# The first MLP product of the last 24 weight tiles as seven 64x64 block products instead of eight

## The chip, the core and the metric

The kernel runs on one core of a Trainium2 chip. TensorE (PE) multiplies, VectorE (DVE), ScalarE (ACT) and GpSimd (POOL) do elementwise work, SyncE (SP) issues most DMA transfers. The metric is the device time of one execution in microseconds (us). The kernel before takes 259.07 us, the median of three runs (259.07, 259.70 and 259.07).

## The reference

```
phi(x)   = outer(S1 x, S2 x), 64 features for each token and head
attn     = (phi(q) . sum phi(k) v) / (phi(q) . sum phi(k) + 1e-6)     # 4 batches, 4 heads, 1088 tokens, head size 32
x        = attn as 4352 tokens by 128
h        = x @ w_in                       # 4352x128 by 128x2048
g        = 0.5 h (1 + erf(h / sqrt 2))
out      = g @ w_out                      # 4352x2048 by 2048x128
```

All of it is in float32. The two products of the MLP (x by w_in, g by w_out) are by far the largest part of the arithmetic. This document calls them the first and the second product.

## The kernel before, in words

**Chunks, tiles, blocks and steps.** The 4352 tokens are eight chunks of 512 tokens (0 to 7) and a last one of 256 (chunk 8, the rests of the four batches). The 2048 hidden features are 16 tiles of 128, and four tiles make a block. One pass of the main loop (L1163) is a step: it makes one hidden tile of one chunk. From chunk 2 on, step t makes tile t mod 16 of chunk t div 16, so step 96 opens chunk 6, step 104 is the middle of chunk 6, step 112 opens chunk 7 and step 128 opens chunk 8. Chunks 0 to 7 with 16 tiles are the 128 w_in tiles of the title.

**What one step does.** `hidden` (L715) multiplies a w_in tile by the chunk's transposed x, as two matmuls of 64 output columns each (the array as two column tiles, "128*64" in the profile) into one of two PSUM banks (`h_ps`). ACT applies GELU to that bank (L728) and writes the tile into the chunk's block. After the last tile of a block `token_sums` (L764) forms four sums of 128x512 of pieces of the block on POOL, each about 1.28 us.

**The second product is already done as seven products for eight.** This is a Strassen-Winograd scheme on a 2x2 block form: halves of the 256 tokens by halves of 128 output columns, over pairs of tiles. Its token side is what `token_sums` makes, its weight side (`T`, `channel_sums`, L749) is made once. `two_products` (L794) issues one pair of products of 128*64 tiles and 256 columns each, into the chunk's two PSUM banks `acc` (`o_ps`). A block has seven such pairs; they are spread over the steps after the block by the table `products` (L1133 to L1161). `drain` (L812) takes the two banks apart once a chunk's products are done: two ACT copies and seven DVE operations, all of which read PSUM and have at most one operand in SBUF. `combine` (L837) adds SBUF to SBUF (L841, L842), and `store` (L860) transposes on DVE and issues the output's DMAs on SP.

**Order.** Every engine runs its instructions in the order in which the text emits them: the loop at L1217 to L1223 ties each instruction to the one before it on its engine. So on DVE, an operation of an earlier step is never overtaken by one of a later step, however late its own inputs are. Within a step the order is: `drain` of that step, `hidden`, the `slots` (functions placed with `at(t, ...)`), `store`, then that step's `products`. For chunk 5 `drain` stands at step 101 and `store` at step 107. `last_attends` at step 95 makes the x of chunks 6, 7 and 8.

**PSUM.** There are eight banks: two `h_ps`, two `o_ps`, and four `w_ps` (two pairs, used by the attention part, which is done by step 95 but for the accumulators of chunk 8).

The lines that tie the order:

```
    last = {}
    for ins in nc.cur_bb.bb.instructions:
        if ins.engine in last:
            tc.add_manual_dep(ins, last[ins.engine].name,
                              mybir.DependencyInfo(mybir.DependencyClass.NoSync, mybir.DependencyReason.DATA),
                              reason="order of the text")
        last[ins.engine] = ins
```

Of the kernel before, what the change touches and what calls it, by code (L numbers as in the profile page):

```python
# [8 lines left out]
FP = mybir.dt.float32  # L9
U32 = mybir.dt.uint32  # L10
AX = mybir.AluOpType
ACT = mybir.ActivationFunctionType
# [4 lines left out]
def kernel(  # L17
# [17 lines left out]
    nc = tc.nc  # L35
    pe, dve, act, pool, sp = nc.tensor, nc.vector, nc.scalar, nc.gpsimd, nc.sync
# [5 lines left out]
    NF = d_ff // 128  # L42
# [5 lines left out]
    CW = JC * 128  # L48
    G = 128 // 32
    NCH = J // JC  # L50
    C = D + 1
    LAG = 2
    NMAIN = B * NCH
    NB = 4
# [6 lines left out]
    att = ctx.enter_context(tc.tile_pool(name="att", bufs=2))  # L61
    mlp = ctx.enter_context(tc.tile_pool(name="mlp", bufs=2))
# [4 lines left out]
    def work_banks():  # L67

        return wps.tile([128, 2, CW], FP, name="w_ps")
# [7 lines left out]
    def hidden_bank():  # L77
        return hps.tile([128, CW], FP, name="h_ps")

    def out_bank():  # L80
        return ops.tile([128, CW], FP, name="o_ps")
# [5 lines left out]
    pieces = list(zip(CUTS, CUTS[1:]))  # L87
# [4 lines left out]
    main = {(n, b): big.tile([128, H, J, D], FP, name=f"{n}_{b}") for n in "kv" for b in range(B)}  # L92
    q_sb = [big.tile([128, H, JC, D], FP, name=f"q_{n}") for n in range(NMAIN)]
    w_in_sb = [big.tile([d_model, c1 - c0], FP, name=f"w_in{i}") for i, (c0, c1) in enumerate(pieces)]
# [42 lines left out]
    def block(dtype=U32):  # L137

        b = big.tile([128, NB, 512], U32, name="block", bufs=3)
        return b if dtype == U32 else b.bitcast(dtype)  # L140
# [46 lines left out]
    for i, s in enumerate((S1, S2)):  # L187
        s, e = words(s)
# [328 lines left out]
    qT, qp, xT = {}, {}, {}  # L517
# [13 lines left out]
    A, B_of = {}, {}  # L531
# [174 lines left out]
    g_of, o_of = {}, {}  # L706

    def w_tile(w, fi):
        i = max(i for i, (c0, c1) in enumerate(pieces) if c0 <= fi * 128)
        at = fi * 128 - CUTS[i]  # L710
        return w[i][:, at:at + 128]
# [3 lines left out]
    def hidden(n, fi, by_halves=False):  # L715
        W = width[n]
        ps = first_banks.pop((n, fi)) if (n, fi) in first_banks else hidden_bank()
        w = w_tile(w_in_sb, fi)
        for rows in (slice(0, 64), slice(64, 128)) if by_halves else (slice(0, 128),):
            if (n, fi) not in begun:  # L720
                pe.matmul(ps[rows, :W], lhsT=w[:, rows], rhs=xT[n][:, :W], start=True, stop=True)  # L721
        if n < NCH and fi < USUAL:
            g_of[n, fi] = mlp.tile([128, CW], FP, name="g", bufs=4)
        else:
            if fi % NB == 0:
                blocks[n, fi // NB] = block(FP)
            g_of[n, fi] = blocks[n, fi // NB][:, fi % NB]
        act.activation(out=g_of[n, fi][:, :W], in_=ps[:, :W], func=ACT.Gelu)  # L728

    def first_hidden(n, half):  # L730
# [4 lines left out]
        for i in range(parts):  # L735
# [5 lines left out]
    blocks, sums, acc = {}, {}, {}  # L741
    T = {}
    HW = CW // 2
    NPAIR = NF // 2

    PLACE = {"1": (0, 0, 0), "2": (0, 0, HW), "3": (1, 0, 0), "5": (1, 0, HW),
             "4": (0, 1, 0), "6a": (0, 1, HW), "7": (1, 1, 0), "6b": (1, 1, HW)}
# [16 lines left out]
    def token_sums(n, b):  # L764

        g = blocks[n, b].rearrange("p (e two) (half x) -> p e two half x", two=2, half=2)
        a11, a21, a12, a22 = (g[:, :, k, h] for k in range(2) for h in range(2))
        s = {}
        for j, (name, dtype) in enumerate((("bits_a", U32), ("bits_e", U32), ("bits_low", FP), ("bits_m", FP))):
            t = mlp.tile([128, LC], dtype, name=name, bufs=3 if dtype == U32 else 2)  # L770
            s[j + 1] = (t if dtype == FP else t.bitcast(FP)).rearrange("p (e x) -> p e x", e=2)
        pool.tensor_sub(out=s[3], in0=a11, in1=a21)  # L772
        pool.tensor_add(out=s[1], in0=a21, in1=a22)  # L773
        pool.tensor_sub(out=s[2], in0=s[1], in1=a11)  # L774
        pool.tensor_sub(out=s[4], in0=a12, in1=s[2])  # L775
        sums[n, b] = s

    def factor(n, b, name, e):

        k = 2 * b + e  # L780
        if name in "12":
            fi = 2 * k + int(name) - 1
            return g_of[n, fi][:, 0:HW], w_tile(w_out_sb, fi)[:, 0:64]
        if name == "3":
            return sums[n, b][4][:, e], w_tile(w_out_sb, 2 * k + 1)[:, 64:128]
        if name == "4":
            return g_of[n, 2 * k + 1][:, HW:], T[4][:, k]
        j = {"5": 1, "6": 2, "7": 3}[name[0]]
        return sums[n, b][j][:, e], T[j][:, k]

    def first_block(n):
        return USUAL // NB if n < NCH else 0

    def two_products(n, b, i):  # L794
# [8 lines left out]
        for name, e in zip(two[:2], two[2:]):  # L803
# [3 lines left out]
            pe.matmul(acc[n][bank][half * 64:(half + 1) * 64, col:col + HW], lhsT=fixed, rhs=moving,  # L807
                      start=opens and e == 0 and name in "4715", stop=b == NF // NB - 1, skip_group_check=True)

    drained = {}  # L810

    def drain(n):  # L812
# [79 lines left out]
    bank = work_bank()  # L892
# [74 lines left out]
    def at(t, f, *a):  # L967
        slots[t].append(lambda: f(*a))
# [161 lines left out]
                at(t + 10, turn_first_kv)  # L1130


    products = {t: [] for t in range(len(steps) + LAG)}  # L1133
    done = {t: [] for t in range(len(steps) + LAG + 1)}
    drains = {t: [] for t in range(len(steps) + LAG + 1)}
    for t, (n, fi) in enumerate(steps):
        if n < NCH and fi < USUAL:
            products[t + LAG].append((project, n, fi))
            if fi == USUAL - 1:
                slots[t + LAG + 1 + 2 * n].append(lambda n=n: take_usual(n))  # L1140
        elif n == NMAIN:
            at_ = max(t + LAG, (n * NF + 5) if fi < 3 else (n * NF + 6) if fi < 5 else 0)
            if fi < NF - 4:
                products[at_].append((project, n, fi))
            if fi == NF - 1:

                products[at_] += [(project, n, NF - f, (i,)) for f, i in ((4, 0), (3, 0), (2, 0), (4, 1), (1, 0), (3, 1),
                                                                          (2, 1), (1, 1))]
                done[at_ + 1].append(n)
        elif fi % NB == NB - 1:  # L1150
            b = fi // NB
            opens = b == first_block(n)
            late = int(n < NCH or n == NCH and opens)
            for later, pairs in ((3, 3), (4, 2), (5, 2)) if opens else ((2, 2), (3, 2), (4, 1), (5, 2)):
                later += late
                for i in range(pairs):
                    products[t + later].append((two_products, n, b, len([p for q in products.values() for p in q
                                                                        if p[:3] == (two_products, n, b)])))
            if b == NF // NB - 1:
                drains[t + 6 + late].append(n)  # L1160
                done[t + 12].append(n)  # L1161

    for t in range(len(steps) + LAG):  # L1163
        if t < 4:

            hidden(0, t)
            if t == 1:
                w_out[0].low_words()
                w_out[0].exponents()
                w_out[0].finish()  # L1170
                w_out[1].fields()
            if t == 2:
                w_out[1].low_words()
            if t == 3:
                banks = work_banks()
                numerators_by_token(1, halves(banks), range(JC))
                w_out[1].mantissas(by_pool=True)
                w_out[1].exponents()
                divide(1, banks, range(JC), by_head_pair=False)
                w_out[1].signs()  # L1180
                w_out[1].product()
                project(0, 0)
                project(0, 1, cols=slice(0, 256))
                turn_half(1, 0, work_bank(), by_act)
                project(0, 1, cols=slice(256, 512))
                turn_half(1, 1, work_bank(), by_dve)
            continue
        if t == 4:
            first_hidden(1, 0)
            for f, *a in products[t]:  # L1190
                f(*a)
            first_hidden(1, 1)
        for n in drains[t]:
            drain(n)
        sooner = t == NMAIN * NF
        if sooner:
            for f, *a in products[t]:
                f(*a)
        if t < len(steps):
            n, fi = steps[t]  # L1200
            hidden(n, fi, by_halves=t >= 18 and (n < NMAIN or fi < 5))
        if t < len(steps) and steps[t][0] < NMAIN and steps[t][1] % NB == NB - 1:
            n, b = steps[t][0], steps[t][1] // NB
            if b >= first_block(n):
                token_sums(n, b)
        for f in slots[t]:
            f()
        for n in done[t]:
            store(n)
        if t != 4 and not sooner:  # L1210
            for f, *a in products[t]:
                f(*a)
# [4 lines left out]
    last = {}  # L1217
# [36 lines left out]
```

## Time and profile before

| what | us |
|---|---|
| median of three runs | 259.07 |
| the profiled execution, first to last instruction (its span) | 257.9 |
| PE busy in it | 253.1 |
| POOL busy | 163.6 |
| DVE busy | 151.1 |
| ACT busy | 115.2 |
| step 101 (chunk 6, tile 5) starts on PE | 192.93 |
| step 104 starts on PE | 197.66 |
| step 128 (chunk 8) starts on PE | 237.26 |

The profile is one execution. All times in it are counted from its first instruction. The profiled execution's own time is its span and what lies around it (launch and the last transfer's end): the median is 1.2 us above the span. A matmul of float32 shows as two records, one for each of its passes, and a record is longer than the time until the next one may start, because matmuls are pipelined. "PEld" is the loading of weights, which runs beside the matmuls.

### The profile page before, as it was taken

What the parts mean: (1) busy time and instruction counts of PE and PEld (TensorE: products, weight loads), DVE (VectorE), ACT (ScalarE), POOL (GpSimd) and SP (SyncE); (2) the same over time, 40 slices, a digit from 0 to 9 for tenths busy, and PEclk for the clock granted to TensorE, in tenths of its full rate; (3) what the DMA queues carried; (4) which work ended last, traced back from release to release, by engine and by line L of the source; (5) the groups of instructions that cost most, each with busy time, mean ns of one, the idle gap of its engine ahead of it and who ended that gap; (6) DMA issues with size and microseconds to landing.
All of it is one profiled execution on the core that took longest, in us unless ns stands there. A gap on an engine that the chain in (4) does not pass through costs nothing.

```text
span 257.9 us, 5770 instructions
## 1 busy us (share of the span) xinstructions
PE 253.1 (98%) x2335; PEld 135.5 (53%) x2335; DVE 151.1 (59%) x313; ACT 115.2 (45%) x224; POOL 163.6 (63%) x173
## 2 busy tenths in 40 slices
PE   8989999999999999999999999999999999999995
PEld 7846444354444545444444455455544444445794
DVE  3786888969699997590178986399307000700330
ACT  4665777433626332543335332533444334433442
POOL 3313006799968778587758775787758777877300
PEclk9999999999999999999999999999999999999999
DMA  6459747751000101102000002000200200020020
GB/s 203 143 156 375 181 117 174 211 131 15 4 0 13 29 3 23 20 8 35 3 0 3 0 10 37 0 1 3 41 3 5 38 0 1 7 36 0 3 41 20
DMA packets 29594, 13.48 MB, mean 52 GB/s; under 512 B 21888, under 2 KB 27776, under 8 KB 29568
## 3 DMA queue, kind: packets, MB, share of 16 engines
q1 hardware_dynamic: 29392, 13.05, 20.2%
q8 instruction: 18, 0.29, 0.5%
q10 hardware_dynamic: 176, 0.07, 0.1%
q14 instruction: 8, 0.07, 0.1%
HBM read 10.88 MB, written 2.23 MB: 51 GB/s over the span
## 4 chain that ended last, share of the span: by engine, by line
PE 93%; SPq 2%; DMA 2%; DVE 1%; issue 0%; ACT 0%
PE h_ps L721 45%; PE o_ps L807 33%; PE o_ps L858 5%; PE w_ps L855 3%; DMA small<-in_moe_w_in_dram 2%; PE w_ps L437 1%; PE w_ps L578 1%; PE w_ps L633 1%; SPq L132 1%; PE h_ps L737 1%; SPq L100 1%; PE w_ps L977 1%; PE w_ps L656 0%; SPq L118 0%; PE w_ps L467 0%
## 5 line engine op out<-in xcount | busy, mean ns | idle before, releaser
L721 PE MATMUL h_ps<-xT,w_in 128*64 128x512 f32 (+3 forms) x514 | 136.9, 576 | 0.0
L728 ACT ACTIVATE block<-h_ps 128x512 f32<-128x512 f32 (+1 forms) x128 | 73.1, 571 | 117.2 <-PE h_ps L721 115.3
L721 PEld LDWEIGHTS h_ps<-xT,w_in 128*64 128x64 f32 (+1 forms) x514 | 41.9, 142 | 30.5 <-issue 11.6
L807 PE MATMUL o_ps<-block,w_out 128*64 128x256 f32 x224 | 57.5, 379 | 0.0
L772 POOL TENSOR_TENSOR bits_low<-block 128x512 f32<-128x512 f32 x28 | 36.0, 1286 | 27.7 <-ACT block L728 27.7
L807 PEld LDWEIGHTS o_ps<-block,w_out 128*64 128x64 f32 x224 | 30.5, 137 | 38.0 <-issue 27.5
L773 POOL TENSOR_TENSOR bits_a<-block 128x512 f32<-128x512 f32 x28 | 35.8, 1278 | 11.8 <-ACT block L728 11.8
L822 DVE COPY sums<-o_ps 64x256 f32<-64x256 f32 x8 | 3.3, 417 | 60.6 <-PE o_ps L807 60.6
L774 POOL TENSOR_TENSOR bits_e<-bits_a,block 128x512 f32<-128x512 f32 x28 | 36.1, 1288 | 2.2
L775 POOL TENSOR_TENSOR bits_m<-block,bits_e 128x512 f32<-128x512 f32 x28 | 35.9, 1282 | 2.2
L807 PE MATMUL o_ps<-bits_a,small 128*64 128x256 f32 x112 | 28.8, 379 | 0.0
L807 PE MATMUL o_ps<-bits_low,small 128*64 128x256 f32 x112 | 28.8, 379 | 0.0
L807 PE MATMUL o_ps<-block,small 128*64 128x256 f32 x112 | 28.8, 379 | 0.0
L807 PE MATMUL o_ps<-bits_m,w_out 128*64 128x256 f32 x112 | 28.7, 379 | 0.0
L807 PEld LDWEIGHTS o_ps<-block,small 128*64 128x64 f32 x112 | 15.2, 137 | 17.9 <-issue 10.8
L807 PE MATMUL o_ps<-bits_e,small 128*64 128x256 f32 x112 | 17.0, 383 | 0.0
L858 PE MATMUL o_ps<-g,w_out 128*128 128x512 f32 (+1 forms) x34 | 16.5, 572 | 0.0
L807 PEld LDWEIGHTS o_ps<-bits_m,w_out 128*64 128x64 f32 x112 | 15.3, 137 | 0.0
L807 PEld LDWEIGHTS o_ps<-bits_a,small 128*64 128x64 f32 x112 | 15.2, 137 | 0.0
L807 PEld LDWEIGHTS o_ps<-bits_low,small 128*64 128x64 f32 x112 | 15.2, 137 | 0.0
L590 DVE STREAM_TRANSPOSE w_ps<-w_ps 128x512 f32<-128x512 f32 (+1 forms) x7 | 4.8, 687 | 17.1 <-ACT xT L644 12.7
L807 PEld LDWEIGHTS o_ps<-bits_e,small 128*64 128x64 f32 x112 | 7.7, 137 | 10.6 <-issue 8.8
(195 smaller groups left out, 303.7 us busy)
## 6 DMA issues: line engine op xcount, KB each, us to landing
block<-in_moe_w_in_dram SPq DMA_DIRECT2D x3, 512.0 KB, 11.3
block<-in_moe_w_out_dram SPq DMA_DIRECT2D x3, 512.0 KB, 14.7
k<-in_k_dram SPq DMA_DIRECT2D x12, 128.0 KB, 2.9
v<-in_v_dram SPq DMA_DIRECT2D x12, 128.0 KB, 3.5
q<-in_q_dram SPq DMA_DIRECT2D x24, 64.0 KB, 2.1
out_dram<-oT SPq DMA_DIRECT2D x21, 64.0 KB, 2.2
k<-in_k_dram SPq DMA_DIRECT2D x2, 256.0 KB, 2.8
q<-in_q_dram SPq DMA_DIRECT2D x2, 256.0 KB, 3.9
```

The source lines that it names most:

```text
L100: eng.dma_start(out=main[n, b][:, heads], in_=src_of[n][b, heads, 0:MAIN, :].rearrange("h (p j) d -> p h j d", j=J))
L590: dve.transpose(out=tok, in_=ps[:, :, :H2])
L721: pe.matmul(ps[rows, :W], lhsT=w[:, rows], rhs=xT[n][:, :W], start=True, stop=True)
L728: act.activation(out=g_of[n, fi][:, :W], in_=ps[:, :W], func=ACT.Gelu)
L772: pool.tensor_sub(out=s[3], in0=a11, in1=a21)
L773: pool.tensor_add(out=s[1], in0=a21, in1=a22)
L774: pool.tensor_sub(out=s[2], in0=s[1], in1=a11)
L775: pool.tensor_sub(out=s[4], in0=a12, in1=s[2])
L807: pe.matmul(acc[n][bank][half * 64:(half + 1) * 64, col:col + HW], lhsT=fixed, rhs=moving, start=opens and e == 0 and name in "4715", stop ...
L822: dve.tensor_copy(out=N[lo, 0, one], in_=a0[lo, one])
L855: pe.matmul(o_of[n][i][:, :128], lhsT=g[:, i * 128:(i + 1) * 128], rhs=w_tile(w_out_sb, fi), start=first, stop=final)
L858: pe.matmul(o_of[n][:, cols], lhsT=w_tile(w_out_sb, fi), rhs=g[:, cols], start=first, stop=final)
```

## The change

For six blocks, chunk 6's blocks 2 and 3 and the four of chunk 7, the first product is also made as seven 64x64 block products for eight: halves of w_in's 128 rows by halves of a tile pair's columns. All matmuls of both products in these six blocks are on 64x64 tiles of the array.

- `swap_weights` (step 64): ten DMAs on SP copy w_in with its upper and lower 64 partitions swapped. `weight_sums` (steps 93, 94, 98, 98, 99): four DVE additions for each of the five pieces of w_in, all from SBUF to SBUF, 12 of them of 128x256 and eight of 128x128.
- `swap_x` (step 96, chunks 6 and 7): two DMAs on SP each. `x_sums` (chunk 6 at step 102, chunk 7 at step 103): five DVE additions of 128x256 each, SBUF to SBUF.
- `seven_group` replaces four steps of `hidden`. It goes twice (k = 0 and 1) over: seven rounds, each of a hidden block product on one half of the rows (both column halves) and a second product's half on the other half of the rows, of the block two before (`outs_with`). The first four rounds hold the seven hidden products. `pair_ones` copies product 1 on ACT, `pair_sums` adds the seven up with four DVE operations (three of 128x512, one of 128x256) into SBUF, and `pair_gelu` applies GELU to 128x1024.
- The seven products lie in one set of six PSUM banks (the two `h_ps`, the four `w_ps`). Products 3 and 4 of both k share one bank.
- `drain_apart` takes chunk 6's accumulators apart: three ACT copies and one DVE addition release the banks; five more DVE additions (SBUF to SBUF) wait in the list `between`, of which two are emitted after each `pair_sums`.
- The second products of chunk 7's blocks 2 and 3, and those of chunk 8, move to later steps; the drain of chunk 7 moves from step 133 to 137.

```
+    def quarter_products(n, b, names, es, rows):
...
+            pe.matmul(acc[n][bank][half * 64:(half + 1) * 64, col:col + HW], lhsT=fixed[rows], rhs=moving[rows],
+                      start=first, stop=b == NF // NB - 1, skip_group_check=True)
+            ins = nc.cur_bb.bb.instructions[-1]
+            if was not in (None, rows.start):
+                tc.add_manual_dep(ins, seen[0], ..., reason="the other rows' products of this bank")
...
+    def weight_sums(i):
...
+        dve.tensor_add(out=s1, in0=w[:, :, 1], in1=o[:, :, 1])
+        dve.tensor_sub(out=s3, in0=w[:, :, 0], in1=w[:, :, 1])
+        dve.tensor_sub(out=s2, in0=s1, in1=o[:, :, 0])
+        dve.tensor_sub(out=s4, in0=w[:, :, 0], in1=s2)
+    def swap_x(n):
+        xs[n] = mlp.tile([128, CW], FP, name="g", bufs=4)
+        for to, of in ((LO, HI), (HI, LO)):
+            sp.dma_start(out=xs[n][to], in_=xT[n][of])
+    def x_sums(n):
...
+        dve.tensor_sub(out=t[:, 1], in0=sb, in1=sa)
+        dve.tensor_sub(out=t[:, 2], in0=b, in1=t[:, 1])
+        dve.tensor_sub(out=t4, in0=a, in1=t[:, 2])
+        dve.tensor_sub(out=t[:, 0], in0=b, in1=a)
+        dve.tensor_sub(out=t[:, 3], in0=sb, in1=b)
+        XS[n] = {"1": a, "2": a, "3": b, "4": t4, "5": t[:, 0], "6": t[:, 2], "7": t[:, 3]}
+    def pair_product(n, b, k, name):
+        rows, p = pair_rows(k, name), 2 * b + k
+        x, to = XS[n][name], seven[k][name]
+        for e in range(2):
...
+            pe.matmul(to[e * 64:(e + 1) * 64], lhsT=w[rows, e * 64:(e + 1) * 64], rhs=x[rows], start=True, stop=True)
+    def pair_sums(n, b, k, one):
...
+        dve.tensor_add(out=c[:, 0::3], in0=ps["26"], in1=one[:, None, :].broadcast_to([128, 2, HW]))
+        dve.tensor_add(out=u, in0=ps["57"], in1=c[:, 3:4].broadcast_to([128, 2, HW]))
+        dve.tensor_add(out=c[:, 3], in0=ps["57"][:, 0], in1=u[:, 1])
+        dve.tensor_add(out=c[:, 1:3], in0=ps["34"], in1=u)
+    def seven_group(n, b, m, mb):
...
+        for k, (one, two) in enumerate(((LO, HI), (HI, LO))):
+            first = hid(k, "157") + outs([B0] + Bs, one)
+            second = hid(k, "2634") + outs(A, two)
+            both = list(zip(first, second))
+            for i, x in enumerate(both[:4]):
+                for f, *a in x if k == 0 else x[::-1]:
+                    f(*a)
+                if i == 0:
+                    p1 = pair_ones(k)
+            if k == 0:
+                held_gelu()
+            else:
+                pair_gelu(n, b, 0, c)
+            c = pair_sums(n, b, k, p1)
+            for _ in range(2):
+                if between:
+                    between.pop(0)()
+            for x in both[4:]:
...
+        after.append(lambda: (pair_gelu(n, b, 1, c), token_sums(n, b)))
+    def drain_apart(n):
...
+        act.copy(out=A0, in_=a0)
+        act.copy(out=C[lo, 0], in_=a1[hi])
+        act.copy(out=N[hi, 0, one], in_=a1[hi, one])
+        dve.tensor_add(out=C[lo, 1], in0=a1[lo], in1=C[lo, 0])
...
+    outs_with = {(6, 2): (6, 0), (6, 3): (6, 1), (7, 0): (6, 2), (7, 1): (6, 3), (7, 2): (7, 0), (7, 3): (7, 1)}
+    at(64, swap_weights)
+    for i, t in ((3, 93), (4, 94), (0, 98), (1, 98), (2, 99)):
+        at(t, weight_sums, i)
+    for n in range(NMAIN - 2, NMAIN):
+        at(96, swap_x, n)
+        at(102 + n - 6, x_sums, n)
...
+                for later, pairs in ((6, 2), (7, 2), (8, 1), (9, 2)):
...
+                    drains[137].append(n)
+                    done[139].append(n)
```

## The prediction

> **What bounds the kernel now.** I read first the page's busy times and its chain of work, then the timeline of PE, DVE and POOL around step 101, where the change begins to differ.
>
> ```profile
> PE 253.1 (98%) x2335; PEld 135.5 (53%) x2335; DVE 151.1 (59%) x313; ACT 115.2 (45%) x224; POOL 163.6 (63%) x173
> ...
> PE 93%; SPq 2%; DMA 2%; DVE 1%; issue 0%; ACT 0%
> ```
>
> PE never rests, and 93% of the chain is PE: a matmul less is time less, as long as nothing makes PE wait. So the question is who may make it wait. The stretches just before the change and within it:
>
> ```profile
> 182.90:193.10 10.20, 10.20 (x128) 5.46 (x128) 0.02 (x1) 5.08 (x10) 6.86 (x7) 1.00 0.17 27
> 199.50:235.50 36.00, 36.00 (x248) 17.55 (x246) 4.99 (x10) 14.13 (x24) 27.92 (x23) 1.00 0.10 16
> ```
>
> The columns are the stretch, then busy PE, PEld, DVE, ACT, POOL. DVE looks free (0.02 of 10.2 us, 4.99 of 36), POOL is 67% and 78% busy. But POOL's and DVE's adds are not independent. From the timelines of POOL and DVE:
>
> ```profile
> 149.22 1.28 POOL L774 TENSOR_TENSOR bits_e<-bits_a,block 128x512 f32<-128x512 f32 x1
> 150.58 1.33 POOL L775 TENSOR_TENSOR bits_m<-block,bits_e 128x512 f32<-128x512 f32 x1
> ...
> 149.71 1.06 DVE L841 TENSOR_TENSOR sums<-sums 64x256 f32<-64x256 f32 x1
> 150.79 1.40 DVE L842 TENSOR_TENSOR sums<-sums 64x256 f32<-64x256 f32 x1
> ```
>
> A DVE add of two SBUF operands that starts while a POOL sum runs ends 0.27 us after that sum's end (150.50 to 150.77, 151.91 to 152.19); free of POOL the same line takes 0.42 (at 245.70). So beside a busy POOL, DVE gets one such add per POOL sum, every 1.41 us. Adds that read PSUM are not held: L823 has 0.68 beside POOL.
>
> **The gain.** One pair of 256 columns takes 0.43 us of PE (L807 at 192.07, 192.50, 192.93). A block costs four tiles of 0.86 and seven pairs of 0.43, 6.45 us. In the change it is 14 rounds of four 64x64 matmuls. If a round takes 0.43, a block takes 6.02, and six blocks save 2.6 us. Do four small tiles run abreast?
>
> ```profile
> 182.86 1.09 PE L633 MATMUL w_ps<-q_pT,kz 64*32 64x256 f32 x32
> ```
>
> These are 32 records on eight 64x32 tiles; 1.09 us less the last one's tail of 0.17 is 0.92, against 0.86 for two full-speed rounds. They do, and I take 0.43. The Trainium skill, TensorE: Matmul & The Clock Gate (Packing small matmuls, measured speedup), speaks against this: packing four row tiles gave 3.07 times, not four. Were a round 4/3.07 longer, 84 rounds would cost 11 us more. This row packs rows and columns without that loss, so the rule gets no term. The change of tile shape costs 0.1 us twice (the gap ahead of L633, 182.76 to 182.86).
>
> **DVE's preparation, the largest term.** It all stands in DVE's text order: store of chunk 4 (ends 182.92), 20 weight sums, drain of chunk 5, five x sums of chunk 6, five of chunk 7, then the first `pair_sums`. All 30 preparing adds have two SBUF operands.
>
> ```profile
> 182.21 0.71 DVE L869 STREAM_TRANSPOSE oT<-sums 128x512 f32<-128x512 f32 x1
> 193.15 0.42 DVE L822 COPY sums<-o_ps 64x256 f32<-64x256 f32 x1 [10.22 <-PE o_ps L807]
> ...
> 189.95 1.27 POOL L772 TENSOR_TENSOR bits_low<-block 128x512 f32<-128x512 f32 x1 [2.32 <-ACT block L728]
> 191.67 1.27 POOL L773 TENSOR_TENSOR bits_a<-block 128x512 f32<-128x512 f32 x1 [0.45 <-ACT block L728]
> ```
>
> Weight sums: from 182.92 to 187.9 POOL has four sums, and DVE gets five adds. POOL then rests until 189.95: five more adds at 0.44 (256 columns) or 0.31 (128). Ten are left, and POOL now has eight sums, one after the other but for one gap at 191.3: both blocks of chunk 6. One add per sum and one in the gap, so the last ends after the eighth sum, 191.67 + 7 x 1.41 = 201.5, plus an add of 0.44: 202. Unhindered they would take 12 x 0.44 + 8 x 0.31 = 7.8 us and end at 190.7. Then the drain (193.15 to 196.31 before, 3.2 us) ends at 205.3 (196.3 unhindered). POOL is by then out of work, so the x sums run at 0.44: product 5's operand, the fourth, is there at 207.1, the fifth at 207.5, those of chunk 7 at 209.7.
>
> PE gets there much earlier. The pairs of chunk 6's block 0 leave steps 102 to 104, so steps 101 to 103 are three bare tiles: 192.93 + 3 x 0.86 = 195.51. Round 0 needs no sums. Round 1 needs product 5: PE waits from 195.94 to 207.2, 11.3 us. Rounds 1 to 6 and two of k = 1 bring it to 210.6; round 2 of k = 1 overwrites the bank of products 3 and 4, which the last add of `pair_sums` reads. That chain (three at 0.68, one at 0.43, gaps: 2.6 us) starts behind the x sums at 209.7 and ends at 212.3: another 1.8 us. Entry: **+13.1**. Unhindered by POOL: x sums from 196.3, wait until 198.2 (2.2 us), chain from 200.9 to 203.5 (1.9): +4.1.
>
> A second rule: the same page of the Trainium skill (The HAM clock gate) halves PE's clock after an idle window of 3.4 us. This profile grants full speed in all its slices, but its first padding matmuls (L890) take 656 ns against 398 for a warm one of that size (L737). By the rule the first four rounds after the wait would take double, 1.7 us more, and PE would reach round 2 of k = 1 at 212.3 instead of 210.6. By either the sum is the same, since DVE's chain ends at 212.3.
>
> **The steady state.** A half (k) is seven rounds, 3.01 us. ACT copies product 1 by 1.0 us after the half's start, DVE's chain runs from 1.06 to 3.66, and the next half's round 2 comes at 3.87. That holds with 0.1 to 0.2 us to spare; every further 0.4 us of DVE work in a half fits, and what is more delays PE one for one. If a handover costs 0.3 more than I think, each of ten halves loses 0.2: bounds 0 to +2; I take 0. GELU of 1024 columns (1.02 us by 385 ns for 256 and 598 for 512) and the copies fill half of ACT. The change adds a wait: the first second-product of a half on each bank waits for that copy, with all later rounds behind it on PE; it stands in round 3, at 1.29, so it has 0.3 us to spare, and ACT's GELU of the half before starts only behind the copy. POOL's four sums (5.4 us with gaps) fit in a block's 6.02, and their readers come two blocks later.
>
> **Other DVE work in the halves.** The store of chunk 5 (step 107) comes behind `pair_sums` of block 2: two SBUF adds and a transpose of 0.71, 1.65 us with POOL idle (it waits for GELU), less the room: **+1.0** (up to +2 beside POOL). The drain of chunk 6: ACT's copies 0.58, 0.58, 0.40, then the DVE add 0.68 release the second bank 2.2 us after the group, which wants it at 1.72: +0.45. The copy of product 1 queues behind these three copies, so the DVE chain is 1.1 late: +0.5 in the next half. Of the five waiting adds two come after each `pair_sums`, and POOL is then at work on chunk 7's block 1: 1.35 and 1.40 instead of 0.44 each. The next chain is late by that much less the room, +2.35; the next two adds and the last find POOL nearly idle: +0.55. Sum **+3.9** (+2.0 if POOL holds none of them).
>
> **Moved at no cost, and what covers it.** SP's ten swaps at step 64 and four at step 96 issue at 0.65 each (L884: 1.30 for two), land in about 2.1, and delay SP's store DMAs by 2.6 us at step 96; nobody on PE waits for stores. If they were late, chunk 6's x sums start later than 190, still far before DVE gets to them. ACT's queue: 128 GELUs become 104 and 12 wide ones, less work. POOL's sums move behind the wide GELU (`held_gelu`): if that came late, pairs wait two blocks on; the cover is 0.6 us. The later pairs of chunks 7 and 8 are as many rounds as before. The end is PE's second products of chunk 8, DVE's drain of chunk 7 at step 137 is 10 us ahead of it.
>
> **Sum.** -2.6 + 0.2 (two changes of tile shape) + 13.1 + 1.0 + 3.9 = +15.6 on a span of 257.9, so 273.5; the median was 1.2 above the span: **274.7 us**. Measurements of this kernel tell no change from one below 0.3%, about 0.8 us.
>
> **Rivals.**
> 1. DVE is late but POOL does not hold its preparing adds, because POOL loses the turns instead. For it: at 181.75 a DVE add kept its 0.42 and the POOL sum took 1.39. Against it: both adds at 149.71. Price: entry 4.1, store 1.0, drain 2.0: 259.07 - 2.4 + 7.1 = 263.8.
> 2. Faster: DVE does the x sums before chunk 5's drain, that is, its order is not the text's. It decides from this point: product 5's operand ready by 195.9. Then the entry costs nothing, and the rest hides if the adds are spread: 259.07 - 2.4 = 256.7. For it: x is on hand from 185.4 and DVE idle for 10 us. Against it: the loop that ties each instruction to the one before.
> 3. The small tiles lose a quarter or the spare 0.2 us is not there: DVE's lateness is then partly hidden under slower rounds, but the steady state adds 3 to 5: 278.
>
> **How the numbers follow.** Forecast (270 to 277) 0.54, rival 1 (261 to 269) 0.22, rival 2 0.17, rival 3 (above 277) 0.05, and 0.02 for no difference. The range 261 to 278 leaves out rival 2, the case of no difference and part of rival 3, 0.2 in all; its ends are rival 1 with its store and drain cheaper, and the forecast with +2 of steady state and +1 of store. Faster is rival 2, 0.17; same 0.02; slower 0.81.
>
> **What would show it.** PE idle of about 11 us near 196 released by a DVE sum of x, and a smaller one near 211 released by the last add of `pair_sums`; L822 of chunk 5 near 202 instead of 193; weight sums of 1.3 to 1.4 us beside POOL; rounds of 0.43 elsewhere; small PE waits after step 107 and in chunk 7's blocks 2 and 3. I am wrong if DVE has finished the x sums near 196, if the adds take 0.44 beside POOL, or if records of 64*64 lie 0.5 us apart.

## The result, and the profile after

The kernel after takes 271.97 us (median of four runs, 271.22 to 272.86), against 259.07 for the kernel before in the same measurement: ratio 1.049, with an interval of 1.0465 to 1.052. It is 12.9 us slower; 274.7 was forecast. The profiled execution is the quickest of the four, 271.22 with a span of 269.4.

PE's slices, its granted clock and the chain of work on the page of the kernel after:

```profile
PE 255.5 (95%) x2751; PEld 146.9 (55%) x2751; DVE 199.1 (74%) x390; ACT 117.9 (44%) x225; POOL 164.6 (61%) x173
...
PE   8999999999999999999999999999908999989995
...
PEclk9999999999999999999999999999977999999999
...
PE 72%; DVE 18%; issue 4%; SPq 2%; DMA 2%; ACT 1%; DVEq 0%; ACTq 0%
```

DVE, with 1% of the chain before, now holds 18%. One slice of PE is empty (each is 6.7 us), the clock is short of full in it and in the slice behind it, and one more slice near the end of the six blocks is short of full. What PE waited for, in total, times, and the longest:

```profile
PE w_ps L896 <- DVE k L870: 6.9, 1, 6.9
PE h_ps L896 <- DVE v L912: 1.2, 1, 1.2
PE h_ps L896 <- DVE k L912: 0.8, 2, 0.6
```

L896 issues a hidden block product. L870 makes the token operand of product 5. L912 is the last add of `pair_sums`. So the large wait is the forecast one, at another size, and the forecast second wait on `pair_sums` in block 2 of chunk 6 is not in the list.

A half (one k, seven rounds) is measured from the start of its product 1 to the start of the next half's. Seven rounds at the predicted 0.43 are 3.01 us. Halves are named (chunk, block) and k. The first start is at 195.28, and the last half ends where step 128 begins, near 245.5.

| half | (6,2) 0 | (6,2) 1 | (6,3) 0 | (6,3) 1 | (7,0) 0 | (7,0) 1 | (7,1) 0 | (7,1) 1 | (7,2) 0 | (7,2) 1 | (7,3) 0 | (7,3) 1 |
|---|---|---|---|---|---|---|---|---|---|---|---|---|
| us | 11.81 | 2.98 | 3.34 | 3.86 | 3.33 | 2.99 | 3.32 | 2.99 | 3.96 | 3.24 | 4.91 | 3.5 |
| over 3.01 | 8.80 | 0 | 0.33 | 0.85 | 0.32 | 0 | 0.31 | 0 | 0.95 | 0.23 | 1.90 | 0.5 |

The excess is 14.1 us (the undisturbed halves are 0.02 to 0.03 under 3.01). The blocks themselves save 2.6 (84 rounds in place of six times 6.45), so 11.5 is left, which is the whole difference of the two spans (269.4 less 257.9). Outside these halves two small amounts cancel: this execution reaches step 101 0.41 us sooner than the profiled one before (192.52 against 192.93), a lead that it has from its first steps on, and it loses about as much at the change of tile shape into the first half and behind step 128.

DVE before and in the large wait, from its timeline (start, length):

```profile
189.55 1.41 DVE L855 TENSOR_TENSOR v<-w_in,v 128x128 f32<-128x128 f32 x1
...
191.29 0.28 DVE L854 TENSOR_TENSOR v<-k,q 128x128 f32<-128x128 f32 x1
...
192.77 0.41 DVE L852 TENSOR_TENSOR k<-w_in,q 128x256 f32<-128x256 f32 x1
...
196.05 1.37 DVE L855 TENSOR_TENSOR v<-w_in,v 128x256 f32<-128x256 f32 x1
197.34 0.41 DVE L990 COPY sums<-o_ps 64x256 f32<-64x256 f32 x1
...
200.40 1.11 DVE L867 TENSOR_TENSOR k<-g 128x256 f32<-128x256 f32 x1
201.54 0.42 DVE L868 TENSOR_TENSOR k<-xT,k 128x256 f32<-128x256 f32 x1
202.00 0.42 DVE L869 TENSOR_TENSOR g<-xT,k 128x256 f32<-128x256 f32 x1
202.34 0.41 DVE L870 TENSOR_TENSOR k<-xT 128x256 f32<-128x256 f32 x1
...
205.05 0.69 DVE L909 TENSOR_TENSOR k<-w_ps,q 128x512 f32<-128x512 f32 x1
```

The weight sums run until 197.4, then comes the drain of chunk 5, which was at 193.15 before, then the x sums, and only then `pair_sums`. POOL's sums beside the weight sums:

```profile
189.54 1.27 POOL L772 TENSOR_TENSOR bits_low<-block 128x512 f32<-128x512 f32 x1 [2.04 <-ACT block L728]
191.26 1.44 POOL L773 TENSOR_TENSOR bits_a<-block 128x512 f32<-128x512 f32 x1 [0.45 <-ACT block L728]
192.77 1.54 POOL L774 TENSOR_TENSOR bits_e<-bits_a,block 128x512 f32<-128x512 f32 x1
```

PE on either side of its wait:

```profile
195.56 0.38 PE L896 MATMUL w_ps<-xT,w_in 64*64 64x256 f32 x2
...
202.81 0.69 PE L896 MATMUL w_ps<-k,k 64*64 64x256 f32 x2 [6.87 <-DVE k L870]
```

A matmul of the same shape has 0.38 before the wait and 0.69 behind it. Product 5 was due 0.43 behind product 1, at 195.71; it came 7.1 later, and the six rounds from there to 207.09 took 4.28 instead of 2.58. 7.1 and 1.7 are the 8.8 of this half. Three stretches by engine (stretch, then busy PE, PEld, DVE, ACT, POOL, granted clock, DMA share, GB/s) show the clock in numbers:

```profile
195.00:203.00 8.00, 1.13 (x14) 0.40 (x16) 7.78 (x14) 1.00 (x3) 6.07 (x5) 0.77 0.00 0
203.00:211.00 8.00, 8.00 (x122) 6.84 (x122) 6.61 (x14) 1.56 (x3) 0.00 (x0) 0.81 0.01 2
211.00:246.00 35.00, 32.67 (x552) 24.05 (x548) 29.42 (x50) 15.30 (x23) 25.31 (x20) 1.00 0.06 10
```

In the first, DVE is busy for 7.78 of 8 us and PE for 1.13: the bound of this stretch has gone from PE to DVE. In the second PE is busy throughout, but at 0.81.

### The profile page after: what moved, and what is told of

It reads as the page before. It is cut to its first block, busy times and chain, and to the rows that moved or that the text cites. A ratio compares the mean times of both kernels' runs of the same rounds, so it can differ in the third digit from the quotient of the medians.

```text
span 269.4 us, 6735 instructions
## 1 busy us (share of the span) xinstructions
PE 255.5 (95%) x2751; PEld 146.9 (55%) x2751; DVE 199.1 (74%) x390; ACT 117.9 (44%) x225; POOL 164.6 (61%) x173
## 4 chain that ended last, share of the span: by engine, by line
PE 72%; DVE 18%; issue 4%; SPq 2%; DMA 2%; ACT 1%; DVEq 0%; ACTq 0%
PE h_ps L721 29%; PE o_ps L807 20%; PE o_ps L1026 5%; PE o_ps L823 4%; PE w_ps L1023 3%; PE w_ps L896 2%; PE h_ps L896 2%; DMA small<-in_moe_w_in_dram 2%; PE w_ps L437 1%; DVE v L854 1%; PE w_ps L578 1%; DVE q L910 1%; DVE k L852 1%; DVE q_f L610 1%; DVE k L853 1%
## 5 line engine op out<-in xcount | busy, mean ns | idle before, releaser
L721 PE MATMUL h_ps<-xT,w_in 128*64 128x512 f32 (+3 forms) x426 | 112.2, 569 | 0.0
L728 ACT ACTIVATE block<-h_ps 128x512 f32<-128x512 f32 (+1 forms) x104 | 58.6, 565 | 93.1 <-PE h_ps L721 89.7
L721 PEld LDWEIGHTS h_ps<-xT,w_in 128*64 128x64 f32 (+1 forms) x426 | 34.8, 143 | 27.8 <-issue 11.4
L807 PE MATMUL o_ps<-block,w_out 128*64 128x256 f32 x176 | 45.2, 379 | 0.0
L807 PEld LDWEIGHTS o_ps<-block,w_out 128*64 128x64 f32 x176 | 24.0, 137 | 29.0 <-issue 20.7
L823 PE MATMUL o_ps<-block,w_out 64*64 64x256 f32 x96 | 23.7, 386 | 0.0
L807 PE MATMUL o_ps<-block,small 128*64 128x256 f32 x88 | 22.7, 380 | 0.0
L807 PE MATMUL o_ps<-bits_a,small 128*64 128x256 f32 x88 | 22.6, 380 | 0.0
L1026 PE MATMUL o_ps<-g,w_out 128*128 128x512 f32 (+1 forms) x34 | 16.5, 572 | 0.0
L823 PEld LDWEIGHTS o_ps<-block,w_out 64*64 64x64 f32 x96 | 13.1, 138 | 0.5
L823 PE MATMUL o_ps<-bits_a,small 64*64 64x256 f32 x48 | 13.1, 395 | 0.0
```

What stands on the lines that cost most here:

```text
L1026: pe.matmul(o_of[n][:, cols], lhsT=w_tile(w_out_sb, fi), rhs=g[:, cols], start=first, stop=final)
```

## The experiments

What had to be told apart: whether the large wait belongs to the weight sums beside POOL, to the x sums, or to both; what the clock costs; whether the 0.3 us in the first halves is a wait of DVE or a slower array; and what sets the end of chunk 6's drain. Nine kernels were run; their ratios are to runs of the kernel before on the same chip (medians 259.25 to 259.5). Halves are given only where they differ from the table above.

### Weight sums earlier

```
-    at(64, swap_weights)
-    for i, t in ((3, 93), (4, 94), (0, 98), (1, 98), (2, 99)):
+    at(46, swap_weights)
+    for i, t in ((3, 62), (4, 62), (0, 62), (1, 62), (2, 62)):
```

> The swaps of w_in move to step 46 and all 20 weight sums to step 62, where DVE is idle for 12 us; the x sums and the drain of chunk 5 stay. Theory A (text order on DVE, and an add of two SBUF operands waits out a POOL sum): the drain of chunk 5 starts at about 192.7 instead of 197.3 and ends at 195.9, but the x sums now fall beside POOL's sums of chunk 6's block 1, which last to 200.2, so the fourth is ready only at about 200.4 instead of 202.7, and the wait for product 5's operand is still 4 to 5 us; 1.5 to 2.5 us less than the changed kernel, about 270. Rival (POOL does not hold the adds; DVE is merely late by the weight sums' own length): the fourth x sum is ready at 198, the wait is 2 us, the clock stays up, and the time falls by 5 us or more, to 267 or less. Rival (the x sums wait for their DMA): no change.

Measured: 272.39 us, ratio 1.050 (1.048 to 1.0516): the expected 1.5 to 2.5 us did not come. The chain in question is in DVE's timeline and PE's waits:

```profile
194.51 0.42 DVE L990 COPY sums<-o_ps 64x256 f32<-64x256 f32 x1 [10.22 <-PE o_ps L807]
...
197.70 0.83 DVE L867 TENSOR_TENSOR k<-g 128x256 f32<-128x256 f32 x1
198.56 1.37 DVE L868 TENSOR_TENSOR k<-xT,k 128x256 f32<-128x256 f32 x1
199.96 1.37 DVE L869 TENSOR_TENSOR g<-xT,k 128x256 f32<-128x256 f32 x1
201.25 1.48 DVE L870 TENSOR_TENSOR k<-xT 128x256 f32<-128x256 f32 x1
```

```profile
PE w_ps L896 <- DVE k L870: 5.1, 1, 5.1
...
PE o_ps L807 <- DVE sums L991: 1.2, 1, 1.2
```

The drain now starts as soon as PE has finished chunk 5's last second product, and the x sums follow at 197.70 instead of 200.40. But POOL is not done with its sums yet:

```profile
199.72 1.33 POOL L774 TENSOR_TENSOR bits_e<-bits_a,block 128x512 f32<-128x512 f32 x1
```

The four adds that took 1.11, 0.42, 0.42 and 0.41 in the kernel after, mostly behind POOL's last sum, take 0.83, 1.37, 1.37 and 1.48 here, for the same operands and shapes. Moved 2.7 us earlier, they end at 202.73 instead of 202.75. That is the hold by POOL, shown by a move of the same instructions. The wait is shorter by 1.8 only because PE comes to it 1.8 later. Most of that is a new wait: 20 adds in a row beside POOL take 16.5 us (115.4 to 131.9), the drain of chunk 3 is late behind them, and PE waits 1.2 for it near 139. Another 0.4 is this execution's lateness from its first steps on.

### x sums earlier, alone and together with the weight sums

With the weight sums left at steps 93 to 99, the halves of x are swapped by ACT copies, and the x sums go to steps 95 to 98:

```
-            sp.dma_start(out=xs[n][to], in_=xT[n][of])
+            act.copy(out=xs[n][to], in_=xT[n][of])
...
+    def x_difference(n):
...
+        dve.tensor_sub(out=t[:, 0], in0=xT[n][:, HW:], in1=xT[n][:, :HW])
...
-        dve.tensor_sub(out=t[:, 0], in0=b, in1=a)
...
-        at(96, swap_x, n)
-        at(102 + n - 6, x_sums, n)
+        at(95, x_difference, n)
+        at(96 + n - 6, swap_x, n)
+        at(97 + n - 6, x_sums, n)
```

> Only the x part of e5: halves of x swapped by ACT, x sums ahead of chunk 5's drain; the weight sums stay at steps 93 to 99. Theory (what counts is that all 30 preparing adds stand ahead of the drain and of the first pair_sums in DVE's text, not which of them): DVE still ends the 30 adds at about 203 and the drain at 206 to 207, so now PE waits for chunk 5's accumulator banks in round 3 of (6,2) rather than for product 5's operand in round 1; the time is that of the changed kernel or up to 2 us more, 271.5 to 274. Rival (the x sums' place alone is the cause): 263.5 to 266.

Measured: 275.09 us, ratio 1.060 (1.0579 to 1.0619), 2.8 us by ratio worse than the kernel after and 1.1 above the range expected; the wait has the expected new place. PE's longest wait, and DVE around it:

```profile
PE o_ps L823 <- DVE sums L994: 8.6, 1, 8.6
```

```profile
204.32 0.43 DVE L855 TENSOR_TENSOR v<-w_in,v 128x256 f32<-128x256 f32 x1
...
205.00 0.67 DVE L994 TENSOR_TENSOR sums<-o_ps,sums 64x512 f32<-64x512 f32 x1
```

All 30 adds now stand ahead of the drain of chunk 5, and end at 204.75. The wait has not become smaller but has another releaser: PE waits for the accumulator banks (L823 is a second product), which the drain releases. PE goes on at 205.7, and the granted clock is one half from 201.48 to 211.72, so that 6.0 us of the slow clock fall on work, against 3.27 in the kernel after. Half of the difference, 1.4 us, is an estimate of what that costs, and would cover the 1.1.

With both moves, the weight sums also spread out (`at(46, swap_weights)`, pieces at steps 62, 62, 62, 66 and 82):

> All preparing adds go where DVE is idle: weight sums of pieces 3, 4 and 0 at step 62, of piece 1 at 66, of piece 2 at 82; the halves of x are swapped by ACT copies (four of 0.58 us) at steps 96 and 97 instead of DMAs, b - a of both chunks is formed at step 95 and the other x sums at 97 and 98, all ahead of chunk 5's drain in DVE's text. Theory A: the x sums end at about 193.2 of the clock of before, when the drain can start; the wait for product 5's operand goes, the clock stays up, the two halves of (6,2) take 3.0 to 3.4 us instead of 11.8 and 3.0; 7.5 to 8.6 us less, 263.5 to 264.5. Rival 1 (the lost time at the entry is the new tile shape or the first use of the six banks, not DVE's order): the halves of (6,2) stay above 6 us.

Measured: 262.97 us, ratio 1.0135 (1.0121 to 1.0149). The first two halves are 3.09 and 3.28 (11.81 and 2.98 in the kernel after), the others as in the table. The last x sum and the drain:

```profile
191.44 1.49 DVE L874 TENSOR_TENSOR v<-g,xT 128x256 f32<-128x256 f32 x1
192.85 0.41 DVE L993 COPY sums<-o_ps 64x256 f32<-64x256 f32 x1
```

The two halves of (6,2) together, the entry, were 8.8 us over 6.02 and are 0.35 over it; by the ratios the gain is 1.0493 less 1.0135, 9.3 us (by the halves 8.4, the profiled execution of the kernel after being its quickest). Either move alone gains nothing, both together gain all of it. So no single one of the two groups of adds is the cause: what counts is that DVE has all 30 behind it by the time the drain of chunk 5 can start. How much of the 8.8 us is POOL's hold and how much the mere length of the adds is not measured, as no run took POOL's sums away; the prediction's estimate for adds that nothing holds was 4.1.

### The clock behind the wait

Fifteen more matmuls, on zeros, into a bank that is overwritten later, stand between round 0 and the wait of (6,2):

```
                 if i == 0:
                     p1 = pair_ones(k)
+                    if (n, b, k) == (6, 2, 0):
+                        for _ in range(15):
+                            noughts = [nc.const_aps.tensor(0.0, [128, m], FP) for m in (128, HW)]
+                            pe.matmul(seven[1]["57"][:, :HW], lhsT=noughts[0], rhs=noughts[1], start=True, stop=True)
```

> While PE would wait for the x sums of chunk 6 it runs 15 matmuls on zeros (128x128 by 128x256, 0.43 us each, 6.5 us in all) into a bank that is overwritten later. They add work and no result. Theory (the wait of 7 us lets PE's clock drop, and the six rounds after it take 4.24 us instead of 2.58, which no other wait covers): the rounds take 2.6 to 3.0 us and the time falls by 1.2 to 1.7 us, to about 270.5. Rival, as I predicted (the DVE chain of the x sums and pair_sums sets the next half anyway): within 0.4 us of the changed kernel.

Measured: 271.18 us, ratio 1.0451 (1.0436 to 1.0467). The granted clock, last but two in each line, and the waits of PE:

```profile
195.00:203.00 8.00, 7.91 (x42) 5.82 (x38) 7.78 (x14) 1.24 (x3) 6.30 (x5) 1.00 0.00 0
203.00:211.00 8.00, 6.97 (x122) 5.60 (x124) 6.91 (x15) 1.71 (x3) 0.00 (x0) 1.00 0.01 2
```

```profile
PE h_ps L896 <- DVE k L912: 1.8, 3, 1.0
```

The clock stays full, the six rounds behind the wait are quick, and PE then waits 1.0 for the last add of `pair_sums`, one wait more than the list of the kernel after has. The median is 0.8 us below the kernel after (1.1 by the ratios, whose intervals just touch), between the theory's 1.2 to 1.7 and the rival's 0.4. The two halves of (6,2) take 10.25 and 4.25, 14.50 in sum, against 14.79 in the kernel after. In two other kernels with the same entry (below) they take 15.61 and 15.44. So the slow clock adds 0.3 to 1.1 us to the time; the rest of what it takes is hidden, because DVE's chain would have made PE wait there anyway.

The traces show why the amount varies. In the kernel after the granted clock is one half for 6.83 us, from 199.25 to 206.08, and PE resumes at 202.81: 3.27 us of the slow stretch fall on work. In the two other kernels the slow stretch is as long, 6.83 us, but begins at 201.14 and 200.68, and 4.95 and 4.73 us of it fall on work.

### The 0.3 us in the first halves

In the kernel after, the first add of `pair_sums` starts 1.6 us after its half, not 1.06. It reads products 2 and 6, but these lie in the same two-bank tile of PSUM as products 5 and 7, which are issued later. The edit gives the two pairs a tile each, and changes nothing else:

```
-                x, y = two[k][:, 0], two[k][:, 1]
+                x, y = two[0][:, k], two[1][:, k]
```

> Products 2 and 6 of both halves share one PSUM tile and products 5 and 7 the other; before, each half had its own tile. The first add of pair_sums starts 1.57 us after its half's start in the changed kernel, not 1.06 as products 2 and 6 and the copy of product 1 would allow. Theory: it waits for product 7, which is written into the same tile's other bank. Then it starts at 1.06 to 1.1 here, the 0.3 us that the first half of blocks (6,3), (7,0) and (7,1) lose go, and the store and drain cost some tenths less: 1.0 to 2.5 us less, about 270. Rival: it waits for something of PE or ACT that the tiles do not change (the pipeline's end, the copy): start stays at 1.57 and the time at 272.

Measured: 271.77 us, ratio 1.0465 (1.0441 to 1.0489), not to be told from the kernel after by time. By halves it can be read: the three of 3.32 to 3.34 are now 3.06, 3.03 and 3.03. The add that starts the chain, in the kernel after (half from 220.59) and in this one (half from 221.01):

```profile
222.17 0.69 DVE L909 TENSOR_TENSOR v<-w_ps,q 128x512 f32<-128x512 f32 x1 [0.85 <-PE w_ps L896]
```

```profile
222.14 0.69 DVE L909 TENSOR_TENSOR v<-w_ps,q 128x512 f32<-128x512 f32 x1 [0.44 <-ACT q L900]
```

At 1.58 it was released by PE, at 1.13 by ACT's copy of product 1, as the prediction had assumed. The 0.9 us won in the three halves are offset by a first half of 12.63 instead of 11.81, as more of the slow clock falls on work in this execution, and by a last half that is 0.4 longer: there one of the waiting adds of chunk 6 (L970) now falls beside a POOL sum and takes 1.45 instead of 0.52.

### The waiting adds of chunk 6 later

```
             c = pair_sums(n, b, k, p1)
-            for _ in range(2):
-                if between:
-                    between.pop(0)()
...
-                    done[t + NF].append(n)
+                    done[t + NF + 1].append(n)
```

The five adds of `drain_apart` then run at step 128, behind the six blocks, and the store of chunk 6 follows them.

> The five adds that chunk 6's drain leaves over are emitted after the last block instead of two behind each pair_sums; the store of chunk 6 follows at step 128. Theory: they hold up the DVE chain, so the last three halves, which took 3.24, 4.91 and 3.5 us, fall to 3.0 to 3.4, and the time by 1.8 to 2.7 us, about 269.6; the first half of (7,2), 3.96, stays, as it waits for ACT's three copies and the one add that free the banks. Rival (all four halves wait for ACT's copies and GELU): less than 0.5 us.

Measured: 270.01 us, ratio 1.0399 (1.0376 to 1.0421). The first half of (7,3) goes from 4.91 to 3.32 and the second from 3.5 to 3.1; (7,2) stays at 3.96 and 3.24. In the kernel after, two of the five adds run at

```profile
234.75 1.20 DVE L970 TENSOR_TENSOR sums<-q 64x256 f32<-64x256 f32 x1
235.88 1.49 DVE L973 TENSOR_TENSOR sums<-q,sums 64x256 f32<-64x256 f32 x1
```

and push the next `pair_sums` to 237.29. So 2.0 of the 3.6 us of the drain are the waiting adds, 1.6 of them these two beside POOL, and the 0.95 of (7,2) is the release of the second bank; the last version below gets 0.71 of it back.

### A version that beats both

First the three edits that helped (both sums earlier, banks apart, adds later) together:

> The edits of e2 (products 2 and 6 in one tile, 5 and 7 in another), e3 (five adds after the last block) and e5 together. Theory: what is left is the store of chunk 5 (about 1.1) and the banks of chunk 6's drain (0.95); -2.4 + 2.1, so 258.5 to 259.8, the same as before within its 0.3%. If the three lost times overlap, that is, if a wait taken away only moves to the next, it stays above 261.

Measured: 259.69 us, ratio 1.001 (0.9995 to 1.0024): no difference from the kernel before. Left over are 0.82 in the second half of (6,3) (store of chunk 5), 0.95 and 0.3 in (7,2) (release of chunk 6's banks). Next the store of chunk 5 in parts, its two adds behind the second `pair_sums` of (6,2), its transpose behind the first of (6,3):

```
+            for _ in range({(6, 2, 1): 2, (6, 3, 0): 1}.get((n, b, k), 0)):
+                held_store.pop(0)()
...
+    at(103, store_in_parts, NMAIN - 3)
```

> As e6, and the store of chunk 5 is cut in three: its two adds come behind the second pair_sums of (6,2), where POOL waits for GELU, its transpose and DMAs behind the first of (6,3). Theory: each part fits or nearly fits the 0.4 us that a half leaves DVE: 0.3 to 0.8 less than e6, 258.0 to 259.2. If the room is not there: the same as e6.

Measured: 258.93 us, ratio 0.9976 (0.9967 to 0.9985); the second half of (6,3) goes from 3.83 to 3.23. Last, ACT's copies of `drain_apart` in the order in which they release the banks, and the third one from SBUF behind the GELU:

```
-        act.copy(out=A0, in_=a0)
         act.copy(out=C[lo, 0], in_=a1[hi])
-        act.copy(out=N[hi, 0, one], in_=a1[hi, one])
+        act.copy(out=A0, in_=a0)
         dve.tensor_add(out=C[lo, 1], in0=a1[lo], in1=C[lo, 0])
+        after.append(lambda: act.copy(out=N[hi, 0, one], in_=C[lo, 0, one]))
```

> e7, and in the drain of chunk 6 ACT copies the second bank first, the third copy is taken from SBUF and stands behind GELU, so the one DVE add starts a copy earlier. Theory (the two halves of (7,2), 3.96 and 3.32 in e7, wait for these banks and for the copy of product 1 behind them): together 0.6 to 0.9 less, 258.0 to 258.4, which is 0.4 to 0.6% below the kernel before. Rival (they wait for the new accumulators' first use or for the tile shape): the same as e7.

Measured: 258.43 us, ratio 0.9964 (0.9951 to 0.9978); (7,2) goes from 3.96 to 3.25. This is the fastest of all, 0.36% below the kernel before. Its interval overlaps that of the version ahead of it, so the gain of this last edit is read from the half and not from the time. The first and the third of the stretches shown above:

```profile
195.00:203.00 8.00, 8.00 (x146) 5.62 (x148) 6.64 (x13) 3.28 (x7) 5.52 (x5) 1.00 0.01 2
...
211.00:246.00 35.00, 35.00 (x510) 24.96 (x501) 28.53 (x45) 17.09 (x31) 24.37 (x19) 1.00 0.06 10
```

PE is busy throughout both, at full clock. In the third, DVE is 82% busy, with work that now lies beside PE's. The eleven halves up to the last take 34.0 us, 0.9 more than 11 times 3.01.

## Why the prediction was right, point by point

**The gain, -2.6: right.** Halves that nothing disturbs take 2.98 to 2.99 in the kernel after and 3.00 to 3.01 in the last version, so a round of four 64x64 tiles takes 0.43. The Trainium skill, TensorE: Matmul & The Clock Gate (Packing small matmuls, measured speedup), states 3.07 times for four row tiles; that loss does not carry over to two row by two column tiles, since a round of 0.56 would make a half 3.92. Four row tiles are shown by no run here. The 0.2 for two changes of tile shape: 0.15 and 0.1 in the rows of the kernel after. The last plain step starts at 194.27 and takes 0.86, and the first 64x64 tile follows at 195.28; the last round's second pass starts at 245.22 and takes 0.21, and the next shape follows at 245.53.

**The entry, +13.1: the right mechanism, 8.8 measured.** The first wait was put too long, and in place of the second came a slow clock.
- The end of the weight sums, put at 202, was 197.4. Failed is the step "one add per sum and one in the gap". When POOL resumed, nine adds were left and not ten. Three passed in POOL's gap (190.81 to 191.26) where I let one pass: adds of 128 columns take 0.28 and start 0.2 apart. One of 256 columns won its turn (192.77, 0.41 us), and the POOL sum that started with it took 1.54 instead of 1.27. So five adds waited for a POOL sum, not eight, and three turns of 1.41 fewer are 4.2 of the 4.6 us; the other 0.4 is the lead of this execution. The first wait was 6.9 instead of 11.3. The lock as such was right: the first experiment moved four adds into POOL's time, and they took 5.05 us instead of 2.36. This agrees with the Trainium skill, SBUF — State Buffer (Who interferes with whom): a DVE instruction with two SBUF inputs and a POOL instruction that reads SBUF shut each other out for a whole instruction, and whoever starts first holds it. Here the add at 192.77 held it, and the others waited.
- The second wait, 1.8, did not come: PE reached it late by the slow clock. I had weighed that and left the sum unchanged, "since DVE's chain ends at 212.3". With a full clock the wait did come, 1.0 us long, and the two halves were 0.3 to 1.1 shorter in sum. So the statement held but for these 0.3 to 1.1 of the clock's 1.7 us.

**The steady state, 0 with bounds to +2: 0.9 measured.** What failed is the step "DVE's chain runs from 1.06". It starts at 1.57, as `pair_sums` also waits for products 5 and 7 in the other bank of its tile. That is more than the room of 0.1 to 0.2, and 0.3 is lost in each undisturbed first half. Shown by the edit that gives them a tile each.

**Store of chunk 5, +1.0: 0.85**, and cut in parts 0.2. **Drain of chunk 6, +3.9: 3.6** (0.95, 0.23, 1.90 and 0.5 for 0.45, 0.5, 2.35 and 0.55). That the sum came so close is in part luck: the first part was twice its size, and the next two were smaller. ACT's three copies start 0.27 behind the start of the half (230.16 and 229.89), which the sum did not count; the rest of the 0.5 stays open. The adds beside POOL took 1.20 and 1.49 for the predicted 1.35 and 1.40.

**Moved at no cost: right.** No wait of PE on a DMA, on SP's queue or on ACT's GELU stands in the list for the six blocks.

**The sum.** -2.6 + 8.8 + 0.9 + 0.85 + 3.6 is +11.55, on 257.9, for a measured span of 269.4; forecast was 273.5. The median lay 2.6 above the profiled span and not 1.2: the profiled execution was the quickest, 0.75 below the median, and its own time is 1.8 above its span. That hides 1.4 of the 4.1 us by which the span was missed, so part of the closeness is luck. The miss itself is the entry (4.3 too much), with 0.9 of steady state on the other side.

**The rivals.** The first (POOL loses the turns) was true in full of one add (192.77), which is not enough for its 263.8. The second (x sums ahead of the drain) needs more than its condition named: with the x sums moved alone, the drain is late in their place (275.09). With the weight sums moved as well the entry does vanish, and the rest had to be spread by hand to reach 258.43, where the rival had 256.7. The third (slow small tiles) is refuted by the halves.

## What to carry to other kernels

Where a change trades PE's work for adds on DVE, its price is not DVE's share of busy time (59% before) but the place of the adds in DVE's fixed order: 30 adds of at most 0.44 us, put just ahead of a drain, cost 8.8 us, and at most 0.35 when they were all done early. DVE adds of two SBUF operands beside POOL instructions that follow each other without a gap are to be counted at POOL's period (here 1.41 us). That is an upper bound: up to three adds passed in one gap, and 20 adds beside POOL took 16.5 us and not 28. Moving them into POOL's time can eat all that the move gains. When moving one of two late groups shows nothing, move both before you drop the idea.

## What the runs showed of the hardware that was not expected

- In the stretch of 8 us that holds PE's wait of 7 us and in the one behind it, the clock was granted at 0.77 and 0.81 of full, and four of the six rounds behind the wait took 0.75 to 0.91 us instead of 0.43. This agrees with the rule of the clock gate that the prediction weighed. What that cost varied between executions with the same instructions at this place: the half took 11.81, 12.63 and 12.46 us. The clock was at one half for 6.83 us in each, but 3.27, 4.95 and 4.73 us of that fell on work.
- Matmuls on zeros during the wait kept the clock full (1.00 in both stretches), and gained only 0.3 to 1.1 us here, since DVE ended last.
- In this program the wait of an add on a PSUM tile of two banks covers the writes to both: the add that needs one pair of products started 0.45 us earlier when the other pair lay in another tile. Whether the chip would allow the earlier start within one tile was not tried.
